# A two-layer linear-attention and MLP kernel on one core: the first loads of x and wk regrouped, the first projections split by wk halves, and all order lists settled again

## The chip, the core and the metric

The kernel runs on one core of a Trainium2 chip. The metric is device time in microseconds (us); lower is better. A profile records one execution: its span goes from the first to the last instruction of the program. Engines are PE (matrix multiply; PEld its weight loads), DVE (vector), ACT (scalar, activation functions), POOL (general purpose), SP (here only an issuer of DMAs).

## The reference

The input x has 2048 tokens of width 512. Two layers are applied, each an attention block A and an MLP block B, both with the same weights in both layers:

```python
x = x + _A_ref(_layernorm(x), A_wqkv, A_wo)     # twice: A, B, A, B
x = x + _B_ref(_layernorm(x), B_w1, B_b1, B_w2, B_b2)

# A: 32 heads of 16
q, k, v = split(x @ wqkv)
phi = lambda t: jnp.where(t > 0, t + 1, jnp.exp(t)) + 1e-6
pq, pk = phi(q), phi(k)
kv = einsum("bhsd,bhse->bhde", pk, v);  z = einsum("bhsd->bhd", pk)
o = einsum("bhqd,bhde->bhqe", pq, kv) / (einsum("bhqd,bhd->bhq", pq, z) + 1e-6)
return o @ wo
# B normalizes once more inside
y = _layernorm(x);  return gelu(y @ w1 + b1) @ w2 + b2     # w1: 512 x 1792
```

## The kernel before, in words

**Tiles.** The tokens are 16 tiles of 128 (numbers 0 to 15), in four chunks of four. Layer 0 begins with chunk 3 (tiles 12 to 15), then 0, 1, 2 (`C0`, line 327). Matmuls are 128x128 weights against 512 (or 256, 128) moving columns in bf16.

**Names.** Every operation has a name, and the lists use them. `xc0` to `xc2` load the chunks after the first; `x0`, `x1`, `x2` load the first chunk in pieces; `wk0`, `wk1` are the halves (by rows of the matrix) of the K part of wqkv, `wq` the Q part. `statsA0_12`, `aggrA0_12`, `cenA0_12`, `yscA0_12` are the statistics, the centring and the scaling of tile 12 for attention of layer 0 (function `norm`, line 706); for tile 13 ACT does the sums (`sumA0_13`, `sqA0_13`), and `negA0_13` makes the negative mean. `powA0_12` is the reciprocal root on POOL. `PTA0_12` transposes a tile on PE, `TA0_0` with a DMA; `tcA0_12` copies the transposed tile out of PSUM. `K0_12` and `Q0_3_0` are projections (four matmuls each; `attn_k`, line 843, and `attn_q`, line 860), followed by `exp`, `relu`, `min` and `phi` operations. `G0_12_0` accumulates the product of the normalized tile and phi(k). After the last tile, `KV`, `M` and `WO` make the attention's output, `RA` adds it to x. `TB0_5` and `PTB0_0` transpose tiles for the MLP, `W10_0_5_0` is layer 0, chunk 0, slice 5 of the first MLP matrix, half 0 (chunk 0 is done in halves of two tiles, hence 28 such operations of 256 columns, 0.4375 us each), `gelu` follows on ACT, `W20_1_0` and `W20_1_7` are the two halves of tile 1's second MLP product, which both need the whole of w2. `b20_0` adds b2 to tile 0 (on POOL or DVE), `RB` the MLP's output, `OD` stores a tile.

**What sets the order.** Each engine runs a list of names written out in `CONF["ORDER"]` (lines 329 on), strictly in that order: an operation that waits holds up everything behind it on its engine. A class `Scheduler` (line 111) replays the lists with a duration for each operation (the number after the lambda in `G.op`) and landing times for the first loads (`LAND`, line 326). From this replay come only the choice of buffers and PSUM banks; semaphore waits follow from the data and the buffers. DMAs are issued by SP (loads, transposes, stores), ACT (`wk1` alone) and POOL (the later weights `wo`, `wv`, `w1_0`, `w1_1`, `w2_0`, `w2_1`, function `late`, line 673). So the durations and landing times in the source do not run on the chip; they decide through the lists and the buffers.

**The start.** SP issues `x0` (tile 12, 128 KB, rows of 1 KB in each partition), `x1` (tile 13), `wk0`, `x2` (tiles 14 and 15, 256 KB), `wq` and the three chunks. ACT issues `wk1` once the memset `ones` on DVE is done. PE runs `warm` (nine matmuls on constants, until 4.2 us), the two transposes of tiles 12 and 13 with a few more such matmuls behind each (`idle0_0`, `idle0_1`), and then the first projections; `K0_12` reads both halves of wk.

The late weights are issued by POOL in the order w2_0, wo, wv, w1_0, w1_1, w2_1, between its own operations; w2_1 follows `powB0_0`.

Of the kernel before, what the change touches and what calls it, by code (L numbers as in the profile page):

```python
# [110 lines left out]
class Scheduler:  # L111
# [12 lines left out]
    def run(self):  # L124
# [14 lines left out]
        for _ in g.ops:  # L139
# [29 lines left out]
            if o.fast and pool_busy > at:  # L169
                dur += pool_busy - at - 60.0  # L170
            if o.fast:
                dve_busy = at + dur
            if e == "pool" and o.sem is None and o.dur > 300.0:
                dur += max(0.0, min(dve_busy - at, 400.0))
                pool_busy = at + dur
# [92 lines left out]
def assign_waits(graph, order, sems, dma_sems):  # L268
# [10 lines left out]
    while len(done) < total:  # L279
        moved = False  # L280
        for e in ENGINES:
# [43 lines left out]
    N_WARM2=1, N_IDLE=[4, 3], XQ='sp', WKQ='sp act', WK1=1,  # L325
    LAND={'x0': 3210, 'x1': 3930, 'wk1': 5300, 'wk0': 6430, 'x2': 6950, 'wq': 8450, 'xc0': 9730, 'xc1': 11020, 'xc2': 12240},
# [5 lines left out]
            "warm PTA0_12 idle0_0 PTA0_13 idle0_1 K0_12 K0_13 PTA0_14 Q0_3_0 Q0_3_2 PTA0_15 K0_14 K0_15 G0_12_0 "  # L332
            "Q0_3_1 G0_13_0 Q0_3_3 G0_14_0 PTA0_1 K0_0 G0_15_0 K0_1 Z0_3 G0_0_0 K0_3 K0_2 Q0_0_2 G0_1_0 Q0_0_0 "
            "K0_8 K0_4 G0_2_0 G0_3_0 K0_6 Q0_0_3 G0_4_0 K0_7 K0_5 K0_10 K0_11 Z0_0 K0_9 Z0_1 Q0_1_2 Q0_1_0 Q0_1_3 "
            "Q0_0_1 Z0_2 G0_5_0 G0_6_0 D0_0_0 D0_0_3 G0_7_0 Q0_1_1 G0_8_0 D0_0_1 G0_9_0 D0_0_2 G0_10_0 G0_11_0 "
            "G0_11_2 D0_1_0 G0_11_1 Q0_2_0 G0_11_3 KV0_0 D0_1_1 KV0_1 KV0_2 D0_1_2 ZR0 KV0_3 Q0_2_1 M0_0 M0_2 M0_1 "
            "M0_3 Q0_2_2 WO0_0_0 WO0_0_1 WO0_0_2 WO0_0_3 D0_1_3 WO0_1_0 WO0_2_0 WO0_3_0 Q0_2_3 WO0_4_0 WO0_6_0 "
            "WO0_7_0 PTB0_0 WO0_5_0 W10_0_5_0 W10_0_1_0 W10_0_7_0 W10_0_9_0 W10_0_6_0 W10_0_3_0 W10_0_2_0 "
            "W10_0_4_0 W10_0_12_0 W10_0_13_0 W10_0_0_0 W10_0_10_0 W10_0_11_0 W20_0_0 W10_0_8_0 W20_1_0 W20_1_7 "
            "W20_0_7 W10_0_8_1 W10_0_1_1 W10_0_7_1 W10_0_9_1 W10_0_5_1 W10_0_12_1 W10_0_0_1 W10_0_3_1 W10_0_11_1 "  # L340
            "W10_0_13_1 W10_1_3_0 W10_1_4_0 W10_1_13_0 W10_1_11_0 WO0_8_0 W10_1_0_0 WO0_9_0 W10_1_2_0 W10_0_6_1 "
            "W10_0_2_1 W10_0_4_1 W10_1_8_0 W10_1_12_0 W10_1_7_0 W10_1_5_0 W10_1_10_0 WO0_11_0 W10_1_6_0 W10_1_1_0 "
            "WO0_10_0 W10_1_9_0 W20_4_0 W20_7_0 W20_7_7 W20_4_7 W20_5_0 WO0_15_0 K1_0 W20_2_0 W20_5_7 W20_6_0 "
            "W20_6_7 K1_1 W10_2_10_0 W10_2_3_0 W10_2_0_0 W10_0_10_1 WO0_14_0 W10_2_13_0 WO0_12_0 W10_2_6_0 "
            "WO0_13_0 W20_2_7 W10_2_11_0 W10_2_5_0 W10_2_8_0 W10_2_7_0 W10_2_1_0 W10_2_4_0 W10_2_2_0 W10_2_9_0 "
            "W10_2_12_0 W20_9_0 W20_8_0 W20_9_7 W20_8_7 W20_3_0 W20_3_7 W20_10_0 W20_11_0 K1_4 K1_2 W10_3_1_0 "
            "W10_3_7_0 W10_3_8_0 W10_3_5_0 W20_10_7 W10_3_0_0 W10_3_3_0 W20_11_7 W10_3_9_0 W10_3_6_0 W10_3_10_0 "
            "W10_3_2_0 K1_3 W10_3_13_0 W10_3_4_0 W10_3_12_0 W10_3_11_0 K1_8 K1_5 G1_0_1 G1_0_3 G1_0_0 K1_6 G1_0_2 "
            "W20_12_0 K1_7 W20_12_7 W20_13_0 W20_13_7 W20_14_0 K1_9 K1_10 G1_1_0 W20_15_0 W20_15_7 W20_14_7 K1_11 "
            "Q1_1_1 Q1_1_0 G1_1_1 G1_1_3 G1_1_2 Q1_0_0 K1_13 K1_12 Q1_1_2 G1_2_1 Q1_0_2 K1_14 K1_15 Q1_0_1 Q1_1_3 "  # L350
            "ZH1 Q1_0_3 Z1_3 G1_2_2 G1_3_1 D1_0_0 ZR1 G1_2_0 D1_0_2 G1_3_2 D1_0_1 G1_3_3 G1_3_0 G1_2_3 Q1_3_0 "
            "KV1_0 KV1_1 Q1_3_1 KV1_2 D1_0_3 Q1_3_2 KV1_3 Q1_2_0 M1_1 M1_0 M1_3 M1_2 Q1_2_1 WO1_0_0 Q1_3_3 WO1_0_1 "
            "WO1_1_0 WO1_0_2 WO1_0_3 WO1_3_0 WO1_2_0 Q1_2_2 WO1_5_0 WO1_4_0 PTB1_1 Q1_2_3 PTB1_0 WO1_6_0 "
            "W11_0_13_0 W11_0_10_0 W11_0_12_0 W11_0_4_0 WO1_7_0 W11_0_0_0 W11_0_5_0 W11_0_7_0 W11_0_1_0 W11_0_3_0 "
            "W11_0_11_0 W11_0_6_0 W11_0_9_0 W11_0_8_1 W11_0_11_1 W11_0_4_1 W11_0_3_1 W11_0_8_0 W11_0_0_1 W11_0_5_1 "
# [177 lines left out]
def build_kernel(nc, A_x, A_wqkv, A_wo, B_x, B_w1, B_b1, B_w2, B_b2, out, conf=None, report=False):  # L533
# [5 lines left out]
    with ExitStack() as es:  # L539
# [828 lines left out]
```

## Time and profile before

| what | us |
|---|---|
| median of 3 runs | 328.6 |
| lowest and highest run | 327.31, 330.21 |
| profiled execution, first to last instruction (span) | 326.2 |
| first useful matmul (transpose of tile 12) | 4.57 |
| first projection, `K0_12` | 6.55 |
| last matmul starts | 323.38 |

For the profiled execution the page gives its span; the runs' times are taken on the device and also hold what lies around the program. A timeline line gives start, length, engine, line of the kernel, operation, output<-input, shape, how many instructions were merged, and in brackets the idle time before it with what ended that. Lengths of matmuls are modelled and overlap: their starts tell more than their lengths. A DMA line of the page gives the time from issue to landing.

### The profile page before, as it was taken

Reading aid. Unit: us, or ns where it says so; the run is one execution under the profiler, and the core shown is the slowest. Engines: PE = TensorE matmul, PEld = TensorE weight load, DVE = VectorE, ACT = ScalarE, POOL = GpSimd, SP = SyncE. Lnnn points to the kernel's source line nnn. Section 1 sums busy time; section 2 is a strip of 40 time slices with the busy share of each in tenths; the row PEclk is TensorE's granted clock in tenths of the full one; section 3 lists DMA queues with packets and bytes.
Section 4 is the critical chain, followed back from the end, with each engine's and each line's share of the span. In section 5 each row is a group of like instructions: output and inputs, shape, how many; then the busy total and the mean of one; then the engine's idle time right before and its main releaser. Section 6 shows DMA issues by size and latency. Waiting matters only on the chain.

```text
span 326.2 us, 4796 instructions
## 1 busy us (share of the span) xinstructions
PE 320.6 (98%) x1724; PEld 158.2 (48%) x1724; DVE 218.7 (67%) x506; ACT 197.5 (61%) x338; POOL 131.2 (40%) x224
## 2 busy tenths in 40 slices
PE   7999999999999999999999999999999999999996
PEld 3444545656544444444444444458644444444453
DVE  4998689989866662535468899999988663300132
ACT  5998889744753387357963395969923553645200
POOL 3465637673238106134139525645811275100000
PEclk9999999999999999999999999999999999999999
DMA  7424662524012400312110200111153233300011
GB/s 239 163 51 92 173 223 62 181 49 81 21 31 48 97 1 2 74 22 55 27 32 19 47 17 0 28 39 36 32 92 72 48 45 69 81 0 2 32 64 50
DMA packets 47028, 20.39 MB, mean 62 GB/s; under 512 B 41948, under 2 KB 45532, under 8 KB 47004
## 3 DMA queue, kind: packets, MB, share of 16 engines
q1 hardware_dynamic: 45676, 15.09, 20.4%
q0 software_dynamic: 1056, 4.72, 4.5%
q10 hardware_dynamic: 272, 0.26, 0.3%
q8 instruction: 14, 0.23, 0.3%
q14 instruction: 10, 0.08, 0.1%
HBM read 8.00 MB, written 2.10 MB: 31 GB/s over the span
## 4 chain that ended last, share of the span: by engine, by line
PE 91%; DVE 4%; DMA 2%; ACT 1%; SPq 1%; issue 1%; ACTq 0%
PE ps L1133 29%; PE ps L1171 26%; PE ps L1101 9%; PE ps L852 9%; PE ps L870 5%; PE ps L953 4%; PE ps L883 3%; PE ps L985 2%; DMA t<-in_A_x_dram 1%; PE ps L1158 1%; DMA t<-yb 1%; DVE t L839 1%; PE ps L1008 1%; PE ps L1077 1%; PE ps L797 1%
## 5 line engine op out<-in xcount | busy, mean ns | idle before, releaser
L1139 ACT ACTIVATE gT<-ps,b1c 128x512 bf16<-128x512 f32 (+1 forms) x140 | 76.9, 601 | 61.2 <-PE ps L1133 60.8
L1133 PE MATMUL ps<-t,w 128*128 128x512 bf16 (+1 forms) x560 | 102.2, 336 | 0.5 <-DMA t<-yb 0.3
L1171 PE MATMUL ps<-w,gT 128*128 128x512 bf16 x434 | 97.3, 379 | 0.0
L1133 PEld LDWEIGHTS ps<-t,w 128*128 128x128 bf16 x560 | 54.4, 98 | 44.5 <-DMA t<-yb 0.7
L1171 PEld LDWEIGHTS ps<-w,gT 128*128 128x128 bf16 x434 | 42.4, 98 | 50.4 <-ACT gT L1139 0.3
L822 ACT ACTIVATE eb<-ps 128x512 bf16<-128x512 f32 x56 | 32.1, 606 | 21.3 <-PE ps L852 20.3
L749 POOL TENSOR_TENSOR rstd<-veps,neghalf 128x1 f32<-128x1 f32 x64 | 36.7, 581 | 8.2 <-DVE veps L747 5.5
L1181 DVE TENSOR_TENSOR outb<-ps,xsb 128x512 bf16<-128x512 f32 x15 | 10.3, 689 | 40.3 <-PE ps L1171 32.1
L734 DVE BATCH_NORM_STATS2 stats<-xsb 128x6 f32<-128x512 f32 x48 | 32.0, 681 | 0.2
L1101 PE MATMUL ps<-gtb,t 128*128 128x512 bf16 x128 | 31.8, 379 | 0.1
L852 PE MATMUL ps<-wqkv,t 128*128 128x512 bf16 x128 | 31.1, 379 | 0.0
L769 ACT ACTIVATE yb<-xsb,nmr,rstd 128x512 bf16<-128x512 f32 x21 | 16.8, 811 | 12.6 <-POOL nmr L766 12.5
L833 ACT ACTIVATE rb<-ps 128x512 bf16<-128x512 f32 x38 | 22.3, 611 | 1.6 <-PE ps L852 0.9
L739 POOL TENSOR_SCALAR veps<-mv 128x1 f32<-128x1 f32 x32 | 7.3, 227 | 38.4 <-DVE mv L736 36.6
L774 DVE TENSOR_SCALAR yb<-xsb,mv,rstd 128x512 bf16<-128x512 f32 x27 | 15.0, 572 | 9.0 <-POOL rstd L749 8.9
L835 DVE TENSOR_SCALAR eb<-eb 128x512 bf16<-128x512 bf16 x46 | 13.6, 306 | 10.9 <-ACT eb L822 10.8
L1118 POOL TENSOR_TENSOR xsb<-xsb,b2b 128x512 f32<-128x512 f32 x14 | 17.0, 1218 | 8.1 <-DVE yb L774 6.5
L870 PE MATMUL ps<-wqkv,t 128*128 128x512 bf16 x80 | 20.2, 379 | 0.0
L747 POOL TENSOR_SCALAR veps<-mv 128x1 f32<-128x1 f32 x28 | 8.4, 305 | 28.0 <-DVE mv L736 26.9
L1101 PEld LDWEIGHTS ps<-gtb,t 128*128 128x128 bf16 x128 | 12.3, 98 | 14.9 <-ACT gtb L966 0.7
L852 PEld LDWEIGHTS ps<-wqkv,t 128*128 128x128 bf16 x128 | 12.0, 97 | 14.7 <-ACT t L807 0.9
L1065 POOL TENSOR_TENSOR t<-t,rr 128x512 bf16<-128x512 bf16 x7 | 7.7, 1100 | 24.4 <-DVE rr L1061 14.1
(103 smaller groups left out, 398.7 us busy)
## 6 DMA issues: line engine op xcount, KB each, us to landing
w<-in_B_w_dram POOLq DMA_DIRECT2D x4, 896.0 KB, 5.9
out_dram<-outb SPq DMA_DIRECT2D x15, 128.0 KB, 2.1
t<-in_A_x_dram SPq DMA_DIRECT2D x3, 512.0 KB, 7.3
t<-yb SPq DMA_TRANSPOSE x56, 2.5
wqkv<-in_A_wqkv_dram SPq DMA_DIRECT2D x1, 512.0 KB, 5.7
wo<-in_A_wo_dram POOLq DMA_DIRECT2D x1, 512.0 KB, 6.6
wqkv<-in_A_wqkv_dram POOLq DMA_DIRECT2D x1, 512.0 KB, 4.5
t<-t SPq DMA_TRANSPOSE x20, 2.5
```

Of the source, the lines that this page charges most:

```text
L734: G.op("dve", lambda e: e.bn_stats(stats[:, s.slot, :], src()), 620, reads=src_keys, writes=[k + "s"], tiles=[s, *src_tiles], prio=prio, n ...
L749: G.op("pool", lambda e: e.tensor_tensor(rstd[:, s.slot:s.slot + 1], veps[:, s.slot:s.slot + 1], neghalf[:], op=ALU.pow), 570, reads=[k + ...
L769: G.op("act", lambda e: e.activation(yb[:, y.slot, :], src(), ACT.Identity, bias=nmr[:, s.slot:s.slot + 1], scale=rstd[:, s.slot:s.slot + 1]),
L822: G.op("act", lambda e: e.activation(eb[:, et.slot, :], bank(bt), ACT.Exp, scale=factor()), 478, reads=[src_key, *more], writes=[f"e{tag}" ...
L833: G.op("act", lambda e: e.activation(rb[:, rt.slot, :], bank(bt), ACT.Relu, scale=factor()), 478, reads=[src_key, *more], writes=[f"r{tag} ...
L852: ins = e.matmul(bank(b), lhsT=yTa(yT)[:, dt, k * P:(k + 1) * P], rhs=wqkv[:, dt, D:2 * D], start=(dt == 0), stop=(dt == DT - 1))
L870: ins = e.matmul(bank(b), lhsT=yTa(yT)[:, dt, k * P:(k + 1) * P], rhs=wqkv[:, dt, 0:D], start=(dt == 0), stop=(dt == DT - 1))
L1101: ins = e.matmul(bank(wb), lhsT=yTa(pq)[:, kt, k * P:(k + 1) * P], rhs=gtb[:, kt, :], start=(kt == 0), stop=(kt == DT - 1))
L1118: G.op("pool" if on_pool else "dve", lambda e: e.tensor_tensor(xsb[:, st, :], xsb[:, st, :], b2b[:], op=ALU.add), 1120 if on_pool else 600 ...
L1133: ins = e.matmul(bank(b, n), lhsT=w1[:, dt, ft * P:(ft + 1) * P], rhs=yTa(yT)[:, dt, k0 * P:k1 * P], start=(dt == 0), stop=(dt == DT - 1))
L1139: G.op("act", lambda e, ft=ft, b=b, k0=k0, k1=k1, n=n: e.activation(gT[:, g.slot, ft * 512 + k0 * P:ft * 512 + k1 * P], bank(b, n), ACT.Ge ...
L1171: ins = e.matmul(bank(b), lhsT=gT[:, g.slot, ft * 512 + k * P:ft * 512 + (k + 1) * P], rhs=w2[:, ft, :], start=(ft == 0), stop=(ft == FT - 1))
```

## The change

The first load covers tiles 12 and 13 in one DMA (rows of 2 KB in each partition), both halves of wk follow it on SP (K rows 0 to 255, then 256 to 511), then x2 and wq as before; ACT issues no load. K0_12 and K0_13 become two operations of two matmuls each, one for each half of wk, into the same bank. The replay's rules for DVE and POOL working at the same time and some durations are different, and all lists are new. The assignment of operations to engines (`WAY`) is the same.

```diff
 class Scheduler, run
-            if o.fast and pool_busy > at:
-                dur += pool_busy - at - 60.0
             if o.fast:
+                dur += max(0.0, pool_busy - at - 130.0)
                 dve_busy = at + dur
-            if e == "pool" and o.sem is None and o.dur > 300.0:
-                dur += max(0.0, min(dve_busy - at, 400.0))
-                pool_busy = at + dur
+            if e == "pool" and o.sem is None:
+                dur += max(0.0, dve_busy - at - 130.0)
+                if o.dur > 700.0:
+                    pool_busy = at + dur
 CONF
-    N_WARM2=1, N_IDLE=[4, 3], XQ='sp', WKQ='sp act', WK1=1,
-    LAND={'x0': 3210, 'x1': 3930, 'wk1': 5300, 'wk0': 6430, 'x2': 6950, 'wq': 8450, 'xc0': 9730, 'xc1': 11020, 'xc2': 12240},
+    N_WARM2=1, N_IDLE=[4, 3], XQ='sp', WKQ='sp sp', WK1=0, K_SPLIT=2, K_SPLIT0=0,
+    LAND={'x0': 3450, 'wk0': 4900, 'wk1': 5800, 'x2': 6500, 'wq': 7950, 'xc0': 9250, 'xc1': 10550, 'xc2': 11800},
 pe
-            "warm PTA0_12 idle0_0 PTA0_13 idle0_1 K0_12 K0_13 PTA0_14 Q0_3_0 Q0_3_2 PTA0_15 K0_14 K0_15 G0_12_0 "
+            "warm PTA0_12 idle0_0 PTA0_13 idle0_1 K0_12_0 K0_12 K0_13_0 K0_13 Q0_3_0 PTA0_14 Q0_3_1 PTA0_15 G0_12_0 "
...
-            "WO0_7_0 PTB0_0 WO0_5_0 W10_0_5_0 W10_0_1_0 W10_0_7_0 W10_0_9_0 W10_0_6_0 W10_0_3_0 W10_0_2_0 "
-            "W10_0_4_0 W10_0_12_0 W10_0_13_0 W10_0_0_0 W10_0_10_0 W10_0_11_0 W20_0_0 W10_0_8_0 W20_1_0 W20_1_7 "
+            "PTB0_0 WO0_7_0 WO0_5_0 W10_0_0_0 W10_0_5_0 W10_0_3_0 W10_0_2_0 W10_0_4_0 W10_0_6_0 W10_0_1_0 W10_0_13_0 "
+            "W10_0_10_0 W10_0_11_0 W10_0_7_0 W10_0_12_0 W20_1_0 W10_0_9_0 W10_0_1_1 W10_0_6_1 W10_0_8_0 W10_0_12_1 "
...
 act
-            "wk1 sumA0_13 tcA0_12 sqA0_13 tcA0_13 reluk0_12 expk0_12 tcA0_14 expk0_13 reluk0_13 expq0_3_0 tcA0_15 "
+            sumA0_13 tcA0_12 tcA0_13 sqA0_13 reluk0_12 expk0_12 expk0_13 reluk0_13 tcA0_14 reluq0_3_0 tcA0_15
 dve
-            ones statsA0_12 aggrA0_12 cenA0_12 negA0_13 cenA0_13 vepsA0_12 yscA0_12 statsA0_14 aggrA0_14 cenA0_14
+            statsA0_12 aggrA0_12 cenA0_12 vepsA0_12 negA0_13 cenA0_13 ones yscA0_12 statsA0_15 statsA0_14 aggrA0_15
 pool
-            phik0_6 w2_0 bdm1 wo phiq0_1_2 wv w1_0 phiq0_1_1 pr0_0_2 pr0_1_0 pr0_1_1 w1_1 pr0_1_2 pr0_1_3
-            vepsB0_1 powB0_1 vepsB0_0 powB0_0 w2_1 pz0_2_1 phiq0_2_3 vepsB0_2 powB0_2 vepsB0_3
+            phik0_6 w1_0 wo wv phiq0_1_2 phiq0_1_1 pr0_0_2 pr0_1_0 w2_1 pr0_1_1 w1_1 pr0_1_2 pr0_1_3
+            vepsB0_0 vepsB0_1 powB0_1 powB0_0 b20_0 w2_0 vepsB0_3 vepsB0_2 powB0_3 powB0_2
 sp
-            x0 x1 wk0 x2 wq xc0 xc1 xc2 TA0_0 TA0_3 TA0_2 ... TB0_1 TB0_2 TB0_3 TB0_5 TB0_6 TB0_7 TB0_4 TP0_2_1
+            x0 wk0 wk1 x2 wq xc0 xc1 xc2 TA0_0 TA0_3 TA0_2 ... TB0_1 TB0_3 TB0_2 TB0_7 TB0_6 TB0_4 TB0_5 TP0_2_0
 build_kernel, the first loads
-        dma("sp", lambda e: e.dma_start(x0ap(HC, 0), rows(x_dram, HC)[:, 0, :]), [("x0", FIRST)], [x0[HC]], prio=-120, name="x0", kb=128)
-        for k, n in ((1, 1), (2, 2)):
+        for k, n in ((0, 2), (2, 2)):
 attn_k
+            if L == 0 and c == HC and k < cf["K_SPLIT"]:
+                halves = tuple(range(cf["K_SPLIT0"], len(cf["WKQ"].split()))) + tuple(range(cf["K_SPLIT0"]))
+                for i, h in enumerate(halves):
+                    def part(e, h=h, i=i):
+                        n = DT // len(halves)
+                        for j in range(n):
+                            ins = e.matmul(bank(b), lhsT=yTa(yT)[:, n * h + j, k * P:(k + 1) * P], rhs=wqkv[:, n * h + j, D:2 * D],
+                                           start=(i == j == 0), stop=(i == len(halves) - 1 and j == n - 1))
+                        return ins
+                    G.op("pe", part, DT // len(halves) * MM, reads=[f"yT{L}_{st}", f"wk_{h}"] + ([f"k{L}_{st}"] if i else []), writes=[f"k{L}_{st}"],
+                         tiles=[b, yT], prio=prio, name=f"K{L}_{st}" + (f"_{i}" if i < len(halves) - 1 else ""), lat=MM_DRAIN, n=DT // len(halves), after=after)
 durations of the replay, for instance
-                 570, reads=[k + "v", "neghalf"], writes=[k + "r"], tiles=[s], prio=prio, name=f"pow{tag}")
+                 535, reads=[k + "v", "neghalf"], writes=[k + "r"], tiles=[s], prio=prio, name=f"pow{tag}", lat=45)
```

Other places of the new lists that matter here: all 28 operations of chunk 0 (`W10_0_*`) come before the first of chunk 1 in layer 0 (24 before); in layer 1 `KV1_0` comes behind one more projection, chunk 1 of the MLP begins behind four halves of `W21` (before, seven and a `WO1`), chunk 3 behind nine in a row (before, six); and the last tile's halves `W21_15_h0`, `W21_15_h1` stand together at the end of PE's list.

## The prediction

> **What bounds the kernel now.** I read the page's busy rows first, then the timeline of the first 14 us, the landings of the DMAs, PE's own waits, and the rows of the few operations that the new lists put close to PE.
>
> ```profile
> PE 320.6 (98%) x1724; PEld 158.2 (48%) x1724; DVE 218.7 (67%) x506; ACT 197.5 (61%) x338; POOL 131.2 (40%) x224
> ...
> PE   7999999999999999999999999999999999999996
> ...
> PEclk9999999999999999999999999999999999999999
> ```
>
> PE is full from the second slice to the last, and its granted clock never drops. The number of matmuls does not change (1724 in both programs), so the change can only move three things: when the useful matmuls begin, the few waits between them, and the tail behind the last one. Laid end to end at their own spacing (four of 128x512 take 0.86 us in the chain of waits), the matmuls leave these holes in PE after 8.5 us: 0.41 at 78.81, 0.43 + 0.19 + 0.10 between 203.32 and 210.35, 0.28 at 247.05, 0.42 at 272.07; together 1.83 us. All others are below 0.2 us and I let them stand.
>
> ```profile
> 1.49 0.41 ACTq L657 DMA_DIRECT2D wqkv<-in_A_wqkv_dram  x1
> 2.69 0.43 SPq L660 DMA_DIRECT2D wqkv<-in_A_wqkv_dram  x1
> 3.21 0.69 DVE L734 BATCH_NORM_STATS2 stats<-t 128x6 f32<-128x512 bf16 x1 [1.76 <-DMA t<-in_A_x_dram]
> 4.78 0.63 ACT L722 ACTIVATE eb<-t 128x512 bf16<-128x512 bf16 x1 [2.71 <-DMA t<-in_A_x_dram]
> 6.14 0.40 PE L797 MATMUL ps<-idp,yb 128*128 128x128 bf16 x4 [0.94 <-DVE veps L747]
> 6.55 1.89 PE L852 MATMUL ps<-wqkv,t 128*128 128x512 bf16 x8
> 8.68 1.89 PE L870 MATMUL ps<-wqkv,t 128*128 128x512 bf16 x8
> ```
>
> The start is a chain: tile 13 of x lands late (ACT's sum starts at 4.78, tile 12's statistics at 3.21), so the transpose of 13 stands at 6.14 and the first projection, which waits behind it on PE, at 6.55.
>
> ```profile
> wqkv<-in_A_wqkv_dram SPq DMA_DIRECT2D x1, 512.0 KB, 5.7
> ...
> wqkv<-in_A_wqkv_dram ACTq DMA_DIRECT2D x1, 256.0 KB, 4.0
> wqkv<-in_A_wqkv_dram SPq DMA_DIRECT2D x1, 256.0 KB, 4.5
> ```
>
> Issue plus landing: wk1 (ACT) is there at 5.54, wk0 at 6.24, wq at 8.42; x2 lands at 6.95, so 512 KB of wq took 1.47 us behind it.
>
> **Part 1, the head.** One load of 256 KB replaces two of 128 KB, both wk halves follow on SP; SP still issues five loads up to wq (0.47 us each), ACT issues none. Tile 12: before it landed at 3.19 with 128 KB. From there on the queue moves 256 KB in 0.71 us (wk0 to x2), so another 128 KB cost 0.35: 3.5 (between 3.2, no cost, and 4.76, when x1 landed). Tile 12's chain is then 0.3 later, tile 13's 1.3 earlier. With the rows' spacings from 3.5: statistics, aggregate and centring of 12 end at 4.80, veps and the negated mean at 4.99, centring of 13 at 5.34 (before 6.08), its transpose at 5.40, three idle matmuls, first projection at 5.95, set by the copy of tile 12 on ACT (5.31 to 5.89). Gain 0.6. Both wk halves are needed at 5.95 and 6.38; before, the second stood at 6.24 with x1 and one half ahead of it, now with the same bytes ahead of it, so the split costs nothing while that holds; if a half is late, all of PE stands behind it, for PE runs its list in order. The memset of onesm moves behind tile 13's centring on DVE (0.48), where DVE waits for x2 anyway; without that wait tile 12's scaling and its phi would be 0.5 later, which no matmul before G0_12 needs.
>
> What is late next is wq: the new list puts Q0_3_0 right behind K0_13, at 7.67. The stream of x and wk before had a hole (166 GB/s from 2 to 4 us, 382 from 4 to 6, in the windows). If it closes altogether wq lands near 7.1, if it stays where it is, 8.42. I take 7.9, the middle, nearer to the old row because the first bytes can't come sooner; Q0_3_0 at 8.0, and the set K12, K13, Q, transpose ends at 9.05 against 9.54. With the two ends 7.67 and 8.48 the shift is 0.8 or nothing. I followed the new lists by hand to 16.5 us, where G0_14 stands at 16.46 with its phi ready at 16.4, against 17.15 for the same work before: 0.69 ahead. I book **-0.6** (0 to -0.75). ACT and DVE cover this, and both are nearly full (4.00 and 3.36 of 4 us from 16 to 20): where they can't follow, it is lost.
>
> Beside it, the Trainium skill (DMA: Bandwidth & Descriptors, Issuing engines are not separate DMA queues) holds that issuing from several engines saves only issue time, since all share the same 16 DMA engines. By that rule moving wk1 from ACT to SP brings no byte earlier; the trace agrees as far as x1 took 3.51 us with wk1 under way and x0 2.39 without. By it the head gives 0 in place of -0.6 and the whole comes to 328.2; the late wq below is that case, worked out from rows.
>
> **Part 2, the holes that go.** At 78.81 PE waits for the last transposed tile of chunk 1 (issued 74.74, landed 78.72). The new list puts all 28 half operations of chunk 0 in front, four more of 0.4375, so the first use is at 80.14; but DVE has four or five more 512-wide operations (0.6 each) ahead of the last normalization, which by the same rows ends at 75.55 and queues on SP behind three transposes (1.25 each), issue 77.3, landing 79.8. **-0.4**, with 0.3 left.
>
> At 203.32 to 210: KV1_0 stands one projection (0.86) later in PE's list, with G1_3_0 two matmul groups earlier, so its 0.43 goes. KV1_3 keeps its DVE queue: 24 operations between phik1_14 and gt1_3, 12.3 us before, 12.1 now, PE's cover 13.6 before, 13.4 now. One collision is in these 12.3 us:
>
> ```profile
> L839 DVE TENSOR_TENSOR t<-eb,rb x19: 385/417/1381, 17.6 to 229.6; 128x512 bf16<-128x512 bf16 x19
> ...
> 198.15 1.16 POOL L1053 TENSOR_TENSOR lr<-t,zrow 128x512 f32<-128x512 bf16 x1 [3.55 <-ACT zrow L966]
> ```
>
> The slowest (1381 ns against 417) is the one that runs under POOL's row at 198.15. The new list puts two additions from PSUM at about that place, which were not stretched beside POOL (0.68 at 199.51). Paid again or not, 0 to -0.72; I take **-0.4**.
>
> The Trainium skill (SBUF — State Buffer, Who interferes with whom) says that a DVE instruction with two SBUF inputs blocks against a GpSimd one that reads SBUF, and one with at most one does not. The rows agree; it also lets the three minimums just ahead pay instead, and by that the term would be 0.
>
> At 247.05 and 272.07: chunk 3 has 20.3 us of PE work between WO1_15 and its first use, before 16.8; **-0.6** of 0.70 (0 to -0.70).
>
> **Part 3, what comes close.** Three uses stand at the edge in the new lists.
>
> ```profile
> 59.65 1.23 POOL L674 DMA_DIRECT2D w<-in_B_w_dram  x1
> ...
> DMA to landing us min/median/max: 4.5/5.9/6.6
> ```
>
> (a) w2_0 is now the last weight load, on POOL behind the two powers and b20_0, which waits for normB0_0 (59.85). With b20_0 at 1.2 (line's mean) or 1.6 (its own row) the load starts at 61.1 or 61.5 and lands, by the 896 KB loads of 5.0 to 6.2 us, between 66.2 and 67.7. W20_1_0, which needs it, is at 61.84 + 12 x 0.4375 = 67.09. Cost 0 to 0.6. (b) W10_0_1_1 follows at 69.04; it needs TB0_2, by DVE's rows issued at 66.2, landed at 68.7 with the usual 2.5 us, at 70.2 with the longest, 4.0. Cost 0 to 1.2. (c) In layer 1 chunk 1 is used at 237.2, before 242.8; the last of its transposes (ACT's three normalizations, then SP) lands by the same sums at 237.25. Cost 0 to 0.8. Near the low end for each, 0.3: **+0.9** (0 to 2.6).
>
> Tail: OD11 now goes out between the last tile's halves; issue 0.33, its transfer beside the last one: **+0.1** (0 to 0.3). The other new durations in the source are the planner's and change no instruction.
>
> Sum: -0.6 - 0.4 - 0.4 - 0.6 + 0.9 + 0.1 = -1.0. The profiled span is 326.2, so 325.2 is what its successor should show; the median of the three runs is 328.6, 2.4 above the span, and I keep that distance: **327.6 us**.
>
> **The rivals.** Late wq: the DMA engines are the limit, Q0_3_0 waits until 8.48, the head gives nothing; the 382 GB/s from 4 us on speak for it, the hole before 4 us against: 328.2. Full gain: every edge in part 3 holds; POOL's and DVE's sums have 0 to 0.9 us of slack, but three in a row seldom hold: 326.7. Slower: POOL's list at 59 to 65 us, where b20_0 and the issue of w2_0 now stand ahead of the powers of tiles 2 and 3. If it runs late, w2_0 lands at 68.2 (b20_0 1.6, landing 6.6): 1.1; TB0_2 and TB0_5 follow it, 1.2 each with a long landing. That is 3.5 in place of 0.9, 330.2; it decides from 1.9 us of waits between 66 and 81 us on. For it: TB0_4 already took 3.98 there. Against: the other five transposes took 2.4 to 2.5. That the change does nothing at all is excluded: K0_12 no longer waits for tile 13's late landing.
>
> **How the numbers follow.** Forecast 0.50, late wq 0.20, full gain 0.15, slower 0.15. Cases of both signs hold most of it within 326.7 to 328.6; the forecast's own range is 326.6 to 328.6. The bounds summed are -2.6 and +2.9 (326.0 and 331.5); runs of the kernel before lie from 327.31 to 330.21, so I take 325.6 to 330.3. One per cent, 3.3 us, is about what a measurement tells from no change. No case reaches it alone: faster by more 0.10 (full gain and a lucky run), within 0.78, slower by more 0.12 (the POOL list and a wait that I have not followed between 85 and 180 us).
>
> **What would show it.** Right: statistics of tile 12 at 3.4 to 3.6, first projection at 5.9 to 6.1, first Q at 7.9 to 8.1, no hole at chunk 1's first use in layer 0, none at 272. Wrong: Q at 8.4 or later; a PE wait over 1 us for the w2 load, or for a transpose, between 65 and 81; a hole over 0.7 before KV1_3; any PE hole over 1 us elsewhere.

## The result and the profile after

| what | before | after |
|---|---|---|
| median of 10 runs, us | 328.21 (327.31 to 330.21) | 331.14 (329.99 to 332.82) |
| profiled execution, span | 326.2 | 329.3 |
| first projection starts | 6.55 | 6.39 |
| first Q starts | 8.68 | 8.98 |
| last matmul starts | 323.38 | 326.41 |

The changed kernel is 0.96% slower: ratio 1.0096, 95% interval [1.008, 1.0112]. A second measurement gave 1.0094 [1.0062, 1.0126]. The forecast was 327.6 with a range to 330.3; the time lies above the range.

The page of the changed kernel, the rows that were read first before (busy time, then PE and its granted clock in 40 slices), and the first row of the chain that ended last:

```profile
PE 321.6 (98%) x1724; PEld 159.3 (48%) x1724; DVE 217.8 (66%) x506; ACT 198.7 (60%) x338; POOL 133.5 (41%) x224
...
PE   8999999999999999999999999999999998999996
...
PEclk9999999999999999999999999999999999999999
...
PE 64%; DVE 17%; DMA 5%; POOL 5%; ACT 4%; issue 2%; SPq 2%; DVEq 0%
```

The same row before:

```profile
PE 91%; DVE 4%; DMA 2%; ACT 1%; SPq 1%; issue 1%; ACTq 0%
```

The busy rows hardly tell the two kernels apart. The chain does: PE had 91% of it before, now it has 64%. At each wait of PE the chain goes back into the work of another engine, so the shares tell that the end hangs on more waits; how long PE waits is counted below.

The start, from the timeline of the changed kernel:

```profile
3.46 0.69 DVE L728 BATCH_NORM_STATS2 stats<-t 128x6 f32<-128x512 bf16 x1 [3.46 <-DMA t<-in_A_x_dram]
...
4.82 0.61 PE L791 MATMUL ps<-idp,yb 128*128 128x128 bf16 x4 [0.31 <-DVE veps L741]
...
5.65 0.63 PE L791 MATMUL ps<-idp,yb 128*128 128x128 bf16 x4
...
6.39 2.12 PE L855 MATMUL ps<-wqkv,t 128*128 128x512 bf16 x8
...
8.98 0.82 PE L876 MATMUL ps<-wqkv,t 128*128 128x512 bf16 x3 [0.47 <-DMA wqkv<-in_A_wqkv_dram]
```

Tile 13's transpose now follows at 5.65 without a wait (before 6.14, behind its late load), and the first projection comes 0.16 earlier. But then PE waits for wq until 8.98. The DMA lines say why (KB each, time from issue to landing):

```profile
t<-in_A_x_dram SPq DMA_DIRECT2D x2, 256.0 KB, 3.5
wqkv<-in_A_wqkv_dram SPq DMA_DIRECT2D x2, 256.0 KB, 3.2
wqkv<-in_A_wqkv_dram SPq DMA_DIRECT2D x1, 512.0 KB, 6.2
```

The halves of wk came sooner (3.2 from issue, before 4.0 and 4.5), wq later (6.2, before 5.7): it lands at 8.93 and not at 8.42. By 10 us PE is 0.54 behind the kernel before.

Behind the start the four places where the kernel before waited (1.83 us) are all gone. Others have come: 0.34 at 18.65, 0.65 at 23.16, 0.54 at 36.18, 0.15 at 61.55, 0.86 at 136.60, 0.27 at 238.89, 1.09 at 274.09, 0.45 at 277.57, 0.57 at 287.64, together 4.9 us (measured as before, matmuls laid end to end). 4.9 - 1.83 + 0.54 is 3.6, the span grew by 3.1; gaps below 0.2 us, of which the kernel before had more, make up the rest.

Three of them in the timeline. First the transpose of tile 2 (K0_2 is the matmul at 23.16):

```profile
18.28 1.19 SPq L778 DMA_TRANSPOSE t<-yb  x1
19.52 1.30 SPq L1213 DMA_DIRECT2D b1r<-in_B_b_dram  x1
...
23.16 1.02 PE L846 MATMUL ps<-wqkv,t 128*128 128x512 bf16 x4 [0.48 <-DMA t<-yb]
```

It was issued 1.2 earlier than before (19.46), and landed 1.1 later, at 23.02. Then the gelu (gT in the rows) on ACT:

```profile
133.57 0.27 POOL L760 TENSOR_SCALAR nmr<-mv,rstd 128x1 f32<-128x1 f32 x1
...
133.88 1.52 ACT L763 ACTIVATE yb<-xsb,nmr,rstd 128x512 bf16<-128x512 f32 x2 [2.29 <-POOL nmr L760]
135.30 1.24 ACT L1145 ACTIVATE gT<-ps,b1c 128x512 bf16<-128x512 f32 x2
...
136.60 0.60 PE L1177 MATMUL ps<-w,gT 128*128 128x512 bf16 x2 [0.70 <-ACT gT L1145]
```

ACT stood still for 2.29 us in front of two normalizations whose factor POOL made at 133.57, with two gelus behind them whose inputs were ready. PE needed the second gelu. Last the output buffers:

```profile
266.72 0.68 DVE L1187 TENSOR_TENSOR outb<-ps,xsb 128x512 bf16<-128x512 f32 x1
...
267.72 3.29 SPq L778 DMA_TRANSPOSE t<-yb  x2
271.05 0.58 SPq L1189 DMA_DIRECT2D out_dram<-outb  x1
...
273.34 0.69 DVE L1187 TENSOR_TENSOR outb<-ps,xsb 128x512 bf16<-128x512 f32 x1 [5.28 <-DMA out_dram<-outb]
...
274.06 0.81 SPq L1189 DMA_DIRECT2D out_dram<-outb  x2
274.09 1.69 PE L1177 MATMUL ps<-w,gT 128*128 128x512 bf16 x7 [0.93 <-DVE outb L1187]
```

PE waits for a PSUM bank that RB1_7 must empty (273.34); RB1_7 (outb in the rows) waits 5.28 us for an output buffer, that is for the store of tile 2, which is ready at 267.40 but goes out at 271.05 behind two transposes. There are two output buffers (`NOUT`), and the other one holds tile 1 from 240.2 until 274.4, because the new SP list has OD1 behind OD7.

### The profile page after: what moved, and what is told of

Read it like the earlier page. It is cut to its first block, busy times and chain, and to the rows that moved or that the text cites. A ratio compares the mean times of both kernels' runs of the same rounds, so it can differ in the third digit from the quotient of the medians.

```text
span 329.3 us, 4791 instructions
## 1 busy us (share of the span) xinstructions
PE 321.6 (98%) x1724; PEld 159.3 (48%) x1724; DVE 217.8 (66%) x506; ACT 198.7 (60%) x338; POOL 133.5 (41%) x224
## 4 chain that ended last, share of the span: by engine, by line
PE 64%; DVE 17%; DMA 5%; POOL 5%; ACT 4%; issue 2%; SPq 2%; DVEq 0%
PE ps L1139 22%; PE ps L1177 21%; PE ps L1107 5%; PE ps L846 5%; DVE stats L728 3%; DMA t<-yb 3%; PE ps L959 2%; PE ps L876 2%; POOL rstd L743 2%; PE ps L889 2%; PE ps L991 2%; DVE xsb L1112 2%; DMA wqkv<-in_A_wqkv_dram 2%; ACT yb L763 1%; DVE eb L829 1%
## 5 line engine op out<-in xcount | busy, mean ns | idle before, releaser
L1177 PE MATMUL ps<-w,gT 128*128 128x512 bf16 x434 | 98.6, 379 | 1.6 <-DVE outb L1187 0.9
L743 POOL TENSOR_TENSOR rstd<-veps,neghalf 128x1 f32<-128x1 f32 x64 | 38.6, 611 | 6.6 <-DVE stats L719 3.5
L763 ACT ACTIVATE yb<-xsb,nmr,rstd 128x512 bf16<-128x512 f32 x21 | 16.5, 808 | 25.4 <-POOL nmr L760 24.7
L1107 PE MATMUL ps<-gtb,t 128*128 128x512 bf16 x128 | 30.6, 379 | 0.0
L846 PE MATMUL ps<-wqkv,t 128*128 128x512 bf16 x120 | 29.6, 379 | 0.9 <-DMA t<-yb 0.5
L876 PE MATMUL ps<-wqkv,t 128*128 128x512 bf16 x80 | 20.2, 379 | 0.5 <-DMA wqkv<-in_A_wqkv_dram 0.5
L1124 POOL TENSOR_TENSOR xsb<-xsb,b2b 128x512 f32<-128x512 f32 x14 | 16.5, 1184 | 9.0 <-DVE yb L768 9.0
L1310 ACT ACT_TABLE_LOAD x13 | 16.7, 1283 | 0.2
```

The lines of the kernel that those rows point to most:

```text
L743: G.op("pool", lambda e: e.tensor_tensor(rstd[:, s.slot:s.slot + 1], veps[:, s.slot:s.slot + 1], neghalf[:], op=ALU.pow), 535, reads=[k + ...
L763: G.op("act", lambda e: e.activation(yb[:, y.slot, :], src(), ACT.Identity, bias=nmr[:, s.slot:s.slot + 1], scale=rstd[:, s.slot:s.slot + 1]),
L846: ins = e.matmul(bank(b), lhsT=yTa(yT)[:, dt, k * P:(k + 1) * P], rhs=wqkv[:, dt, D:2 * D], start=(dt == 0), stop=(dt == DT - 1))
L876: ins = e.matmul(bank(b), lhsT=yTa(yT)[:, dt, k * P:(k + 1) * P], rhs=wqkv[:, dt, 0:D], start=(dt == 0), stop=(dt == DT - 1))
L1107: ins = e.matmul(bank(wb), lhsT=yTa(pq)[:, kt, k * P:(k + 1) * P], rhs=gtb[:, kt, :], start=(kt == 0), stop=(kt == DT - 1))
L1177: ins = e.matmul(bank(b), lhsT=gT[:, g.slot, ft * 512 + k * P:ft * 512 + (k + 1) * P], rhs=w2[:, ft, :], start=(ft == 0), stop=(ft == FT - 1))
```

## The experiments

Ratios are to the kernel before on the same chip, with 95% intervals. Diffs show the lists that change.

### Which half of the change: loads alone, lists alone

The new loads with the lists of before:

```diff
-    WKQ='sp act', WK1=1            # loads: x0 x1 wk0 x2 wq, wk1 on ACT
+    WKQ='sp sp', WK1=0             # loads: x0 (256 KB) wk0 wk1 x2 wq, all on SP
```

> The kernel before with its own lists, but with the changed loads (x0 of 256 KB for tiles 12 and 13, then wk0, wk1, x2, wq, all on SP; the projections are not split). Theory A (two separate losses: the loads bring wq 0.5 us later and cost 0.5; the new lists cost the rest, 2.6, in holes of their own): span 326.7 (before 326.2), ratio 1.002, wq lands at 8.9 and the first Q stands at 9.0 or later. Theory B (the loads carry all of it: the later start puts every list out of step, and the holes further on are its shadow): ratio 1.006 to 1.01, holes of 0.5 us and more behind 18 us that the kernel before does not have. Theory C (the loads are neutral or gain, as I predicted; the lists alone lose): ratio 0.998 to 1.000, wq at 8.4 or earlier.

Measured 1.001 [0.999, 1.003]. In its profile the first projection stands at 5.94, as I had forecast (5.95), tile 12 lands at 3.47, but wq at 8.74 and the first Q at 8.78. Theory B falls; between A (1.002) and C (up to 1.000) the ratio doesn't decide.

The new lists with the loads of before (the same diff the other way, on the changed kernel):

> The changed kernel with its new lists and the split projections, but with the loads of before (x0 and x1 of 128 KB, wk1 on ACT; the memset that releases wk1 stands first on DVE again). Theory A: 0.5 below the changed kernel, ratio to before 1.008, the holes at 23, 36, 136 and 274 us are there, the one before the first Q is not. Theory B: without the late start the new lists run as planned, ratio 0.997 to 1.000, no hole over 0.5 us. Theory C: as the changed kernel, ratio 1.0096.

Measured 1.0075 [1.0048, 1.0103], span 329.0. The first Q stands at 8.40 without a wait, and the holes are there all the same: 0.90 at 23, 0.50 at 36, 0.87 at 136, 0.84 at 274, 0.74 at 277, 0.48 at 287. Theory B falls here too: the late start does not make them. The lists carry most of the loss, the loads by themselves at most 0.3%.

### Which part of the lists

Both kernels' lists hold the same names on every engine up to about 213 us, so they can be joined there.

> The changed kernel up to the last transposes of layer 1's chunk 0 (about 213 us), and from there on the order of before on all engines. Up to there the changed kernel lost 0.54 (start) plus 2.39 (holes at 18.65, 23.16, 36.18, 136.60) less 1.13 (holes of before that went, 78.81 and 203 to 210): 1.8. Behind it 2.38 of holes stand against 0.70 of before: 1.7. Theory A: this kernel saves the 1.7, span 327.6, ratio 1.0045. Theory B (a late start shows up somewhere whatever the list): ratio 1.008 to 1.01, other holes take the place of those at 274 to 288. Theory C (the lists' last part is the whole loss): ratio 1.000.

Measured 1.0079 [1.0054, 1.0104]; 249.38 has a hole of 0.68 and 274.73 one of 0.75, which are 0.28 (at 247.05) and 0.42 (at 272.07) in the kernel before. By its number that is theory B; but the kernel with the new lists and no late start, above, has its holes all the same, so a late start isn't needed for them.

> The counterpart of the kernel with the old tail: the kernel before (its loads and its order up to about 213 us), and from there on the new order on all engines. Theory A (the lists lose in both parts, each by its own holes): the holes of the new tail, 0.27 at 239, 1.09 at 274, 0.45 at 277 and 0.57 at 287, stand against 0.70 of before, ratio 1.004 to 1.005. Theory F (the loss sits in the part ahead of 213 us, since the old tail behind the new head saved only 0.2 per cent): ratio 1.001 to 1.002.

Measured 1.0064 [1.0032, 1.0095], more than the 1.004 to 1.005 of theory A, with 1.36 at 274, 0.67 at 277 and 0.54 at 287, and two of 0.25 and 0.29 at 215 and 221. The two parts sum to more than the whole, 0.79 and 0.64 against 0.96%: a list that is spliced to the other's head waits at places of its own. So neither part is free, but the split by parts can't be given better than that. My numbers for the first of the two, a saving of 1.7, were wrong.

### The output buffer

```diff
 sp
-            OD0 ... TB1_12 TB1_13 OD2 TB1_15 OD7 OD1 TB1_14
+            OD0 OD1 ... TB1_12 TB1_13 OD2 TB1_15 OD7 TB1_14
```

> The changed kernel with one name moved: the store OD1 right behind OD0 on SP (its tile is ready at 240.2; in the new list it stands behind OD7 and goes out at 274.4, so that of the two output buffers one is held for 34 us and RB1_7 waits for the store of tile 2). Theory A (the buffer makes the hole of 1.09 at 274.09): that hole goes, and with OD1 (0.44 of SP's time) out of the way of the transpose of tile 14 also the 0.45 at 277.57: ratio 1.005, span 327.9. Rival (the transposes of chunk 3 that land late behind 265 us set the end there, the store only comes with them): the hole at 274 shrinks, but W11_3_13 and W11_2_13 wait as much longer for their transposes, ratio 1.009 as the changed kernel.

Measured 1.0063 [1.0044, 1.0083], span 328.7. Its timeline at the same place:

```profile
263.85 13.76 PE L1177 MATMUL ps<-w,gT 128*128 128x512 bf16 x62
268.14 0.68 DVE L1187 TENSOR_TENSOR outb<-ps,xsb 128x512 bf16<-128x512 f32 x1
269.14 3.43 SPq L778 DMA_TRANSPOSE t<-yb  x2
270.09 0.69 DVE L1187 TENSOR_TENSOR outb<-ps,xsb 128x512 bf16<-128x512 f32 x1 [0.61 <-PE ps L1177]
```

RB1_7 now runs at 270.09 and waits for PE, not for a store; PE goes through 62 matmuls without a break. At 277.78 0.34 is left and the hole at 287 is gone. The two transposes hold SP as long as before (3.43 for issuing the pair, 3.29 in the changed kernel), yet the holes behind them shrink, so the rival falls. One name in a list of DMAs was worth about 0.3% (1.0063 for 1.0096; the intervals just overlap).

### The gelu behind a normalization

```diff
 act
-            gelu0_2_5_0 normA1_2 normA1_6 gelu0_2_11_0 gelu0_2_10_0 expk1_1
+            gelu0_2_5_0 gelu0_2_11_0 gelu0_2_10_0 normA1_2 normA1_6 expk1_1
```

> The changed kernel with two names moved on ACT: the normalizations normA1_2 and normA1_6 stand behind gelu0_2_11_0 and gelu0_2_10_0 and not ahead of them. In the changed kernel ACT waits from 131.59 to 133.88 for POOL's nmrA1_2 (133.57) with two gelus ready behind it, and W20_10_7 waits for the second until 136.60, 0.86 us. Theory A (each hole of the lists costs what it shows): the 0.86 goes and nothing takes its place, ratio 1.0065 to 1.007. Rival (POOL and DVE set the pace there, and what PE wins it loses again before the projections of tiles 2 and 6 or at the transposes of layer 1): ratio 1.009, with a new hole of 0.5 or more between 140 and 210.

Measured 1.0077 [1.0048, 1.0105]. No hole is left at 136, and none came between 62 and 238; the saving against 1.0096 is of the expected size (0.86 us is 0.26%) but inside the intervals.

### Why the transpose of tile 2 lands late

A DMA queue that the page calls "instruction" moves a packet of 16 KB every 15 to 31 us; the start of such a packet is called a fetch here (the last section has the rows).

> The changed kernel with one name moved on SP: the load of b1 goes out behind TA0_6, as in the kernel before, and not right behind TA0_2. In all kernels with the new lists TA0_2 lands 4.7 to 5.6 us after its issue (2.50 in the kernel before) and K0_2 waits 0.65 to 1.50 for it. Theory D1 (the small pieces of the b1 load hold the transpose up): TA0_2 lands 2.5 after its issue, the hole before K0_2 goes, ratio to before 1.007. Theory D2 (the transpose is in flight when the next 16 KB of PE's instructions are fetched, at 19.5 us in the changed kernel, 1.2 us behind the issue): TA0_2 still takes 4.7 or more, ratio 1.009 as the changed kernel.

Measured 1.011 [1.0082, 1.0139]. TA0_2, without the small load behind it, still took 3.94, so b1 alone does not make it late (theory D1 falls); but D2's 4.7 or more did not come either. The fetch began 1.9 us behind the issue here (20.8 and 18.90); in the kernel with the gelus ahead, where it came 1.97 behind and b1 stood there, TA0_2 took 4.90. So b1 may well add to it.

> The changed kernel with the idle matmuls at the start cut otherwise: six of 512 and nine of 128 columns in place of eight of 512 and one of 128, the same number of columns in all, but six matmuls more in PE's program, so that everything PE does comes six matmuls (1.3 us) later in its instruction stream and the fetches of its instructions 1.3 us earlier in time: 18.2 in place of 19.5, 267.2 in place of 268.5. Theory D2: TA0_2 (issued 18.28) lands in 2.5, TB1_12 (issued 267.72) too, so the hole of 0.65 at 23.16 goes and the one of 1.09 at 274.09 shrinks to 0.2 since the store of tile 2 comes 1 us earlier; other transposes, which then are in flight, land 1 to 2 us later, TB0_6 or the one ahead of it near 73 us for one: ratio 1.004 to 1.006. Theory D1: nothing changes, ratio 1.009.

Measured 1.0099 [1.0069, 1.013]. The start was about 1 us later than in the changed kernel's profile, so the first fetch met TA0_2 again (issue 19.10, fetch 19.6, 4.06 to landing). At the other end the forecast held: TB1_12 and TB1_13 took 2.43 and 2.52 (3.86 and 3.36 in the changed kernel), and the hole at 274 shrank from 1.09 to 0.30; TA1_7 (issue 151.42, fetch 152.5) took 3.89 instead, 2.48 in the changed kernel. The time did not follow, so alone this run settles nothing.

### All named places mended

On the new lists with the loads of before:

```diff
 act
+            gelu0_2_10_0 normA1_2 normA1_6     # as above
 dve
-            phiq0_3_3 mink0_4 phik0_4 normA0_11
+            phiq0_3_3 normA0_11 mink0_4 phik0_4
 sp
-            TA0_10 TA0_9 TA0_11
+            TA0_10 TA0_11 TA0_9
+            OD0 OD1                            # as above
-            OD6 TB1_11
+            TB1_11 OD6
```

> The new lists with the loads of before, and with those places mended that the traces named: OD1 goes out behind OD0; normA1_2 and normA1_6 stand behind gelu0_2_10_0 on ACT; normA0_11 stands behind phiq0_3_3 on DVE and TA0_11 ahead of TA0_9 on SP; TB1_11 stands ahead of OD6. Theory A (the holes add up): from the new lists with the loads of before (ratio 1.0075, span 329.0) go 0.87 at 136.6, 0.84 and 0.4 at 274 and 277, 0.4 at 287 and 0.4 at 36, together 2.9: ratio 0.9985 to 1.000; 0.9 at 23 is left. Rival (PE's waits are only moved, since DVE and ACT set the pace): ratio 1.004 or more, with new holes.

Measured 0.9997 [0.9976, 1.0018], span 326.3. From the unmended lists with these loads (330.9, span 329.0) that is 2.4 to 2.7 us for six moved names. The holes at 36, 136, 274, 277 and 287 are gone; 1.05 at 23.22 is left and 0.36 at 81.81 has come. ACT at the place of the gelu:

```profile
130.35 1.26 ACT L1150 ACTIVATE gT<-ps,b1c 128x512 bf16<-128x512 f32 x2 [0.34 <-PE ps L1144]
132.08 1.26 ACT L1150 ACTIVATE gT<-ps,b1c 128x512 bf16<-128x512 f32 x2 [0.46 <-PE ps L1144]
133.88 1.52 ACT L768 ACTIVATE yb<-xsb,nmr,rstd 128x512 bf16<-128x512 f32 x2 [0.54 <-POOL nmr L765]
```

The gelus now end 3.2 earlier (133.34 for 136.54), and the normalizations stand where they stood, at 133.88: they still wait for POOL (nmr in the row), so nothing was paid for it. This kernel keeps the new replay's rules and durations, so the buffers and banks that the replay chose are not what carries the loss.

Then, on top, the transpose of tile 2 out of the fetch's way, by a later normalization:

```diff
 dve
-            mink0_15 normA0_2 phik0_15 statsA0_5 mink0_0 aggrA0_5 phik0_0
+            mink0_15 phik0_15 statsA0_5 mink0_0 aggrA0_5 normA0_2 phik0_0
```

> The mended lists with the loads of before (e10_repair: ratio 0.9997, span 326.3, a hole of 1.05 at 23.22 and one of 0.33 at 18.31) with one name moved on DVE: normA0_2 stands behind phik0_15, statsA0_5, mink0_0 and aggrA0_5, so that the transpose of tile 2 is issued at 19.3 to 19.5 in place of 17.95, behind the start of the fetch of PE's instructions (19.4) and not 1.4 us ahead of it. Theory D2 (a transpose that is in flight when the fetch begins lands late, one issued with or behind it does not): it lands earlier though it is issued later, at 21.9 in place of 23.09; the hole at 23.22 goes, the one at 18.31 too, since phik0_15 comes 0.4 earlier: ratio 0.9955 to 0.997. Rival D3 (the transpose of tile 2 is slow by what it reads or by its place behind the loads): it lands at 24.0 or later, hole of 1.5 to 2, ratio 1.001 to 1.003.

Measured 0.9993 [0.9979, 1.0008], median 327.89, span 325.7. The queue of SP and the projections, K0_3 and K0_2 in one row at 21.03:

```profile
18.98 1.28 SPq L783 DMA_TRANSPOSE t<-yb  x1
20.31 0.61 SPq L1218 DMA_DIRECT2D b1r<-in_B_b_dram  x1
...
21.03 1.89 PE L851 MATMUL ps<-wqkv,t 128*128 128x512 bf16 x8
22.76 1.03 PE L894 MATMUL ps<-t,wqkv 128*128 128x512 bf16 x4
24.21 1.04 PE L851 MATMUL ps<-wqkv,t 128*128 128x512 bf16 x4 [0.43 <-ACT eb L821]
```

Issued 1.0 later, it landed 1.7 earlier (21.40 against 23.09, 2.41 from issue), and the fetch here began at 18.8, ahead of the issue. D3 falls. PE wins the 1.05, and gives 0.59 of it back at 24.21, where a matmul waits for ACT's exponential. This is the fastest kernel measured here, but not distinguishable from the kernel before.

> The kernel with the mended lists and normA0_2 later, with the idle matmuls at the start cut as six of 512 and nine of 128 columns, so that the fetches of PE's instructions come 1.3 us earlier. Theory D2: with the same lists without it, TB0_7 (issued 74.03, fetch at 75.0) and TB1_12 (issued 266.88, fetch at 267.5) land 3.4 and 3.7 after their issue; here the fetches come at 73.7 and 266.2, so both take 2.5, TB0_6, TB0_4 and TB0_5 follow 1.3 us earlier and the hole of 0.36 at 81.81 goes; others, such as TA1_1 (125.45, fetch at 126.1), stay late. Ratio 0.994 to 0.997, 0.2 to 0.5 us below the same lists without it. Rival D3: TB0_7 and TB1_12 stay late, same time.

Measured 1.0014 [0.9997, 1.0031]; TB1_12 took 2.42 as forecast (fetch 265.5, issue 266.34). The hole at 81 is gone, but not by the fetch: the last transpose, TB0_5, landed at 81.03, against 81.11 without the shift, and PE was 0.5 later. TB0_7 took 3.83, because its issue (73.87) was still 0.8 ahead of the fetch (74.7), which came 1 us later than I had worked out. The time did not improve; in this profile wk0 landed at 7.01 and the first projection stood at 7.15, so what the run shows is the transposes, not the time.

### The loads, with one part each and with mended lists

> The kernel before with its own lists and one part of the loads changed: x0 covers tiles 12 and 13 in one load of 256 KB, while wk1 stays on ACT. Theory E1 (wq comes late in the changed loads because all of wk goes through SP's queue, which leaves the transfer of 5 to 6.5 us at 180 to 230 GB/s where the kernel before has 350 to 380): wq lands at 8.4, the first projection stands at 5.95, ratio 0.998. Theory E2 (the 256 KB load with rows of 2 KB is what delays the rest): wq lands at 8.7 or later, ratio 1.001 as with both parts.

Measured 1.0014 [0.9995, 1.0032]; wq at 8.33, but tile 12 at 4.43 and the first projection at 7.39 (in this profile PE's matmuls also ran at half their rate until 9.5). Theory E2 falls by wq, and E1's 0.998 did not come.

> The kernel before with its own lists and the other part of the loads changed: x0 and x1 stay two loads of 128 KB, while wk1 is issued by SP behind wk0. With the 256 KB load alone (wk1 on ACT) wq landed at 8.33, with both parts at 8.5 to 9.4. Theory E1 (all of wk on SP's queue makes wq late): wq at 8.7 or later, tile 12 at 3.2, ratio 1.000 to 1.002. Theory E2 (the 256 KB load does): wq at 8.4, ratio 1.000. In the profiles so far x0 lands at 3.19 and 3.20 as 128 KB and at 3.44 to 4.43 as 256 KB, so either way tile 12's statistics should start at 3.2 here.

Measured 1.0017 [0.9997, 1.0038]; tile 12 at 3.36, wq at 9.52; 0.5 of that is its issue, at 3.19 in place of 2.69, since SP has one load more ahead of it. The wk lines of the two kernels (first the 256 KB load with wk1 on ACT, then two small x loads with all of wk on SP):

```profile
wqkv<-in_A_wqkv_dram SPq DMA_DIRECT2D x1, 512.0 KB, 6.1
...
wqkv<-in_A_wqkv_dram SPq DMA_DIRECT2D x1, 256.0 KB, 3.8
wqkv<-in_A_wqkv_dram ACTq DMA_DIRECT2D x1, 256.0 KB, 5.2
```

```profile
wqkv<-in_A_wqkv_dram SPq DMA_DIRECT2D x2, 256.0 KB, 3.6
wqkv<-in_A_wqkv_dram SPq DMA_DIRECT2D x1, 512.0 KB, 6.3
```

By these profiles, one of each, the large x load goes with a late tile 12, wk on SP with a late wq; why, no run shows. Over all profiles taken, with the loads of before (7) tile 12 lands at 3.19 to 3.80, median 3.29, and wq at 8.25 to 9.06, median 8.47; with all new loads (11) at 3.44 to 4.26, median 4.02, and 8.52 to 9.54, median 9.36.

> The kernel with the mended lists and normA0_2 later, but with the changed loads (x0 of 256 KB, wk0, wk1, x2, wq on SP). Theory E (the changed loads bring tile 12 at 3.4 to 4.4 in place of 3.2 and wq at 8.5 to 9.4 in place of 8.3 to 8.6, so they cost what the first Q waits): 0.3 to 0.8 us above the same lists with the loads of before. Theory G (my prediction's head: tile 13 is there earlier and with it the first projection, -0.6): 0.4 to 0.6 us below it.

Measured 1.0003 [0.9989, 1.0016], median 328.38: 0.5 above the same lists with the old loads (327.89), on the side of theory E; the intervals overlap, but a gain of 0.4 or more, theory G, lies outside what they allow together. No comparison of loads alone separates from zero, but all four lie on the side of a loss, of 0.3 to 0.6 us by their ratios.

> The changed kernel without the split of the first two projections by wk halves (each is one operation of four matmuls again and waits for both halves). Both halves land 1 us and more ahead of the first projection in every profile (5.05 and 6.39 in the changed kernel), so by every theory nothing changes, ratio 1.008 to 1.010. A rival by which the split matters (the second half is late in most runs that were not profiled): 1.011 or more.

Measured 1.0119 [1.0098, 1.0139], higher than expected, but measured apart from the changed kernel. So both were run side by side:

> The changed kernel as it is, once more, on the same chip as the one without the split. If the first comparison holds: ratio 1.008 to 1.011.

> The changed kernel without the split, on the same chip as the changed kernel. Theory (the split changes nothing, both halves are there before the first projection): within 0.1 per cent of the changed kernel beside it. Rival (the split saves 0.2 per cent or 0.7 us in runs in which the second half of wk is late): 0.2 per cent or more above it.

1.0094 [1.0062, 1.0126] with the split and 1.0097 [1.0063, 1.0131] without: the split does nothing that can be measured, and the first value was scatter.

### Moving single operations ahead of the old waits

> The kernel before with its loads and three single moves in PE's list, each one operation more ahead of a place where it waits: W10_0_6_1 ahead of W10_1_3_0 (and its gelu earlier on ACT) for the hole of 0.41 at 78.81, Q1_3_1 ahead of KV1_0 for the 0.43 at 203.32, W21_6_0 ahead of W11_3_2_0 for the 0.42 at 272.07. Theory A (a wait that more work covers is won in full): 1.2 us, ratio 0.996 to 0.997. Rival (the wait comes back at the next use behind it): ratio 0.999 to 1.000.

Measured 1.0004 [0.998, 1.0029]: the rival. One hole of 0.52 stands at 80.77 in place of the 0.41 at 78.81, one of 0.62 at 207.43 in place of 0.43 and 0.19 at 203 and 206, one of 0.75 at 248.83 in place of 0.28, 0.12 and 0.33 at 282 and 287 in place of the 0.42 at 272. PE reaches the next use earlier and waits there. (The profiled execution has 1.55 more at 63.29 behind a transpose of 4.20, TB0_1, whose cause I have not found.)

## Why the prediction was wrong, point by point

- **Head, -0.6: it did not come, and in the profile the sign was wrong.** The step that failed is "I take 7.9" for wq and "3.5" for tile 12. Tile 12 came at 3.44 in the profile, but at 4.02 in the median, and wq at 8.93 and 9.36: later than even my late end of 8.42, since I took the old landing as the worst case. The chain itself was right where its inputs were (5.94 for 5.95 with the old lists); in the changed kernel PE's matmuls still ran at half their rate until 6.9, so that K0_12 stood at 6.39. The price is +0.54 in the profile, and 0.3 to 0.6 us in the comparisons, none of which separates from zero by itself; but a gain of 0.6 (a ratio of 0.998) lies outside each of the three against the kernel before. My "late wq" rival had the right place and too small a price. The rule I weighed beside it, in the Trainium skill (DMA: Bandwidth & Descriptors, Issuing engines are not separate DMA queues), gave 0 and was nearer; it does not give the sign. With wk1 from ACT wq lands at 8.25 to 9.06, with all from SP at 8.52 to 9.54.
- **Holes that go, -1.4: right**, and a little too small; all four places are gone (1.83). At 78.81 I had left 0.3; it did not come in the changed kernel, where PE was late, but it stands in the mended lists (0.36 at 81.81). The stretched operation at 198 did not come again: the slowest of its line took 0.57 in the changed kernel (1.38 before). That an instruction with one SBUF input never pays beside POOL is too wide: a minimum took 0.85 at 176.27 in the kernel before, under an addition on POOL (0.29 in the median).
- **Edges, +0.9: right in place, too large.** (c) cost 0.27. (a) and (b) cost nothing. For (a), w2_0 landed at 68.49, beyond my 67.7, but W20_1_0 stood at 68.75, not at 67.09 (which took the old start of chunk 0). The load moved with PE: in the mended lists with the later normalization it landed at 67.51, and W20_1_0 stood at 68.00, again without a wait. **Tail, +0.1**: +0.02, from the last matmul's start to the end.
- **What was missing, +4.6.** The step that failed is "All others are below 0.2 us and I let them stand" together with "I followed the new lists by hand to 16.5 us". The first is a statement on the old lists; I carried it over to lists in which every neighbour is new. Behind 16.5 us I looked only where the old kernel waited and at three uses that came closer. The waits at 18.65, 23.16, 36.18, 136.60 and 274 to 287 were in no term and no bound (4.9 less (c), 4.6 with the 0.15 at 61.55). Most of the new waits could be read from the lists with the durations of the trace: a store behind a later store on SP, two gelus behind a normalization that POOL feeds late, normA0_11 behind a phi that waits for ACT, TB1_11 behind a store. Undoing these gave back 2.4 to 2.7 us in one kernel, and the holes at their places went, which shows the cause for that part. The hole at 23.16 comes from the transpose and the fetch, not from a duration in the lists, and went when the transpose was moved.
- **The slower rival** had the wrong mechanism: between 65 and 81 us PE waits nowhere. "A wait that I have not followed between 85 and 180 us" exists (0.86), but as one of several; I gave it and a late POOL list together a chance of 0.12, as a loss of over one per cent.
- **The sum**: forecast -1.0; measured +3.1 in the span. +0.54 for -0.6, -1.83 for -1.4, +4.9 for +0.9, the rest small. That the measured 331.14 lies below the 331.5 of my summed bounds is luck: the waits that made it were in none of the terms. Two of my signs of being wrong came, Q behind 8.4 and a hole over 1 us elsewhere (1.09 at 274.09).

## What to carry to other kernels

When an order is settled anew as a whole, the old list of waits says nothing on the new one: walk every engine's list to the end with measured durations, and look above all for an operation that is fed by a slow engine and stands ahead of ready work, and for a store that stands behind later work while it holds one of few buffers. A wait that is covered by moving one operation is won only if the next use of the same engine's output doesn't inherit it. And the latest landing seen in one profile is no upper bound for a load whose queue or size changes.

## What the runs showed of the hardware

**Transposes by DMA and the fetch of instructions.** The page's DMA queues have one of 13 packets (0.21 MB, so 16 KB each), in the changed kernel:

```profile
q8 instruction: 13, 0.21, 0.3%
```

Its packets come every 15 to 31 us, at 19.5, 43.9, 59.7, 75.5 and so on in the changed kernel. I sorted the transposes of all 20 profiles (76 in each, all but that of b1) by the time from their issue to the start of the next such packet:

| packet starts behind the issue by, us | transposes | median from issue to landing, us | over 3.0 us |
|---|---|---|---|
| none near (-1.5 to 2.6) | 1283 | 2.47 | 20 |
| -0.5 to 0 | 38 | 2.61 | 7 |
| 0 to 0.5 | 26 | 2.99 | 13 |
| 0.5 to 1.0 | 32 | 3.47 | 32 |
| 1.0 to 1.5 | 26 | 3.98 | 26 |
| 1.5 to 2.0 | 20 | 4.06 | 20 |
| 2.0 to 2.5 | 32 | 2.48 | 6 |

All 78 transposes behind whose issue such a packet began by 0.5 to 2.0 us took 3.0 to 5.6 us. Why a packet of 16 KB does this, no run shows. SP's issue of the next one can stretch with it: the pair of TB1_12 and TB1_13 in the kernel with the later normalization, and with the fetch moved ahead of it:

```profile
266.25 2.88 SPq L783 DMA_TRANSPOSE t<-yb  x2
```

```profile
266.34 2.50 SPq L783 DMA_TRANSPOSE t<-yb  x2
```

In the first the fetch began at 267.1 and TB1_12 took 3.49, in the second at 265.5 and it took 2.42. So the order of SP and the number of matmuls in the program together go far to decide which transposes are late. That the packets hold PE's instructions is inferred: there are 13 or 14 of them in every profile, for 1724 matmuls (1730 in two kernels), and they came earlier against the work where PE's program had six matmuls more.

**The matmul rate at the start.** Four transposing matmuls at 4.6 to 6.8 us took 0.40 in some profiles and 0.61 in others, spacings of 56 and 107 ns. The change to the fast spacing fell at 3.8 us (before), at 6.9 and at 6.4 in two profiles of the changed kernel, and near 8.9 in the mended lists with the new loads, whose first eight projection matmuls, from 7.10 on, took 2.78 (1.89 at the fast spacing). The row of the granted clock shows none of it; its first slice reads 9 in both kernels. The Trainium skill (TensorE: Matmul & The Clock Gate, Part 1: The HAM clock gate) has a window of about 3.4 us that runs free of the kernel's start, with a transition that varies by ±500 ns under matmuls without a pause. The traces agree with a phase that changes from run to run; here, where PE stood idle for 0.3 to 1.5 us behind the matmuls of `warm`, the change falls between 3.8 and 9.6 us over the 20 profiles.
